# Logits in half steps and q and k for three attention tiles at a time, with an order planned by phase, in a four-layer attention and gMLP kernel

## The chip, the cores and the metric

One core of one Trainium2 chip runs the kernel. The metric is the device time of one execution in microseconds (us). PE is TensorE's matmul row and PEld its weight loads, DVE is VectorE, ACT is ScalarE, POOL is GpSimd, SP is SyncE, which here issues nearly all transfers.

## What is computed

The input x has 2048 rows of 576. Attention A and mixer B alternate, each twice, on the same weights.

```
for two rounds:
    x = x + A(layernorm(x))
    x = x + B(layernorm(x))

A: 32 heads of 18; row s sees keys s, s-2, ..., s-14 (8 keys, 2 apart)
   qkv = x @ wqkv; o = softmax(q . k * 18**-0.5) @ v; return o @ wo
B: z = gelu(x @ w_in)                      # 576 -> 4608
   z1, z2 = halves of z; z2 = layernorm(z2)
   g = w_sp @ z2 + b_sp[:, None]           # over the 2048 rows
   return (z1 * g) @ w_out                 # 2304 -> 576
```

## The kernel before

Five stages follow each other on one core. F0 (`phase_F(0)`) is the first attention and the second half of the first mixer's input product. S1 (`phase_S(1)`) is the mixer's first half and the product over rows with `w_sp`. F2 starts with the mixer's output product (16 row blocks, steps `p3_i`), then does the second attention and again z2. S3 is as S1, and E is the last output product. The change touches F0 and F2 alone.

In an F stage the work is cut into named steps, and class `Flow` puts them in an order. Each step has one or two engines that may take it, a cost, a key (a due time), the steps it comes after, and the buffers that it takes. `Flow.order` keeps a clock for each engine, lets the steps that could start first compete, and takes the one with the least key; a step that stays in the matmul or table mode that the engine is in gets a bonus `STAY`. Then the steps' instructions are issued in that order, so that each engine, and each queue of transfers, works through its list strictly in turn. The costs and keys are numbers in the source: nothing measures them when the kernel is built.

The attention has 18 tiles t of 114 rows (`QT`; 128 with the 14 rows of the window before them). Its steps, with the names that the text uses:

- Layer norm `lnx{i}` (F0), `p3_{i}` (F2), `y{t}` (after the attention): `.s` statistics on DVE, `.p` on POOL, `.n` on ACT, `.t` transpose on PE into `ln_tp`, `.e` copy into the transposed input `xnD`.
- `qk{g}.m0` to `.m4`: q and k of one group of two tiles, 242 columns (`GW`), five blocks of ten matmuls (`mm576`: eight with 128 rows, and two with 64 rows that run side by side). Each block goes to a PSUM tile `qk_ps`, is copied to a staging tile `stg` (`.e0` to `.e4`, six buffers), and written to a bounce tensor in DRAM (`.w0` to `.w4`); step `qk{g}` reads it back in another arrangement into `QK` (three buffers). There are nine groups.
- `v{t}.m`: v of a tile, 20 matmuls on half the array's columns (`v_ps`), and its copy `v{t}`.
- `a{t}.L`: the logits, 64 small matmuls on tiles of 18 rows by 64 columns into two PSUM tiles `L_ps` at once; `.x0` and `.x1` exp on ACT, one for each `L_ps`; `.k` the mask on DVE; `.v` 64 small matmuls into `O_ps`; `.f` divides by the sum (DVE, into `o_t`).
- `w{t}.t` transpose, `.e` copy, `.m0` and `.m1` the product with `wo` (`w_ps`), `.a` the sum with x on DVE, `.w` the store.
- `z{i}.m0` to `.m2`: z2's product for 128 rows, 384 columns each (`z_ps`), `.g0` to `.g2` gelu on ACT, then its layer norm.

All large PSUM tiles come from one ring of three buffers (`H`): `qk_ps`, `v_ps`, `L_ps`, `O_ps`, `w_ps`, `z_ps`, `p3_ps`. The logits of one tile hold two of the three until both exps have read them. Exp and gelu stand in different activation tables; ACT loads a table whenever it goes from one to the other.

The keys before are the same in F0 and F2: a tile's attention has key t (its logits t - 1.2), q and k of group g 2g - 6.5, layer norm ahead of them 2g - 8, v t - 1.5, z2's block i 14.5 + 0.5 i.

Of the kernel before, what the change touches and what calls it, by code (L numbers as in the profile page):

```python
# [11 lines left out]
bf16 = mybir.dt.bfloat16  # L12
# [19 lines left out]
NG = NT // 2  # L32
GW = 2 * QT + HALO
GH = GW // 2
# [6 lines left out]
LX, LW, LR, KQ, KX = 5, 5.0, 6.0, 6.5, 8.0  # L41
# [3 lines left out]
class Flow:  # L45
# [7 lines left out]
    STAY = 0.6  # L53

    def __init__(self, caps):
        self.caps = caps
        self.steps = []
        self.by = {}
        self.users = {}
# [31 lines left out]
    def order(self):  # L91
# [5 lines left out]
        while left:  # L97
# [19 lines left out]
            for e, c in best.items():  # L117
                t0 = max(free.get(e, 0.0), min(t for t, _ in c))
                st = min((st for t, st in c if t <= t0 + 1e-9),
                         key=lambda st: (st["key"] - (self.STAY if self.stays(st, mode.get(e)) else 0), st["n"]))  # L120
                if pick is None or t0 < pick[0]:
                    pick = (t0, e, st)
# [26 lines left out]
class K:  # L149
# [96 lines left out]
    def ln_steps(self, fl, tag, key, row0, n, x, after, uses=(), guard=()):  # L246
# [38 lines left out]
        fl.step(tag + ".s", "DVE", 1.15, key, stats, after, uses, takes=[("ln_st", tag + ".st")])  # L285
        fl.step(tag + ".p", "POOL", 1.2, key, small, [tag + ".s"], [tag + ".st"])
        fl.step(tag + ".n", "ACT", 1.15, key, norm, [tag + ".p"], [tag + ".st", *uses], takes=[("xn", tag + ".xn")])
        fl.step(tag + ".t", "PE", 0.3, key, trans, [tag + ".n"], [tag + ".xn"], takes=[("PT", tag + ".tp")], mode="w")
        fl.step(tag + ".e", ("DVE", "ACT"), 0.72, key, evac, [tag + ".t", *guard], [tag + ".tp"])
# [62 lines left out]
    def phase_F(self, li):  # L352
# [7 lines left out]
        fl = Flow(dict(H=3, PT=2, QK=3, bn=2, stg=6, x=nx, xw=3, xn=3, ln_st=6, o_t=2, oT=2, xb=8))  # L360
# [13 lines left out]
        def QKt():  # L374
            return pool.tile([P, 8, 2, 2, GH], bf16, name="QK", bufs=3)

# [28 lines left out]
        def LNX_steps(i, key):  # L405
            box, tag = {}, f"lnx{i}"

            def load(_):
                box["x"] = pool.tile([P, D], bf16, name="x_in", tag="xb", bufs=8)
                self.dma(box["x"][:], self.A_x[i * P:(i + 1) * P, :])  # L410
            fl.step(tag + ".l", "SP", 0.4, key - 3 if i > 1 else -30, load, takes=[("xb", tag + ".x")], lag=2.2 if i < 2 else LX)
            self.ln_steps(fl, tag, key, i * P, P, lambda: box["x"], [tag + ".l"], [tag + ".x"])
# [8 lines left out]
        def QK_steps(g, key):  # L421
            c0, box, tag = 2 * QT * g, {}, f"qk{g}"

            def opened(_):
                box["bn"] = self.dram.tile([D, 2, 2, GH], bf16, name="qk_bounce", bufs=2)
            fl.step(tag + ".b", "SP", 0.0, key, opened, takes=[("bn", tag + ".bn")])
            for d in range(5):
                M = 126 if d < 4 else 72

                def mm(rest_first, d=d, M=M):  # L430
                    ps = box[d] = self.Ht("qk_ps")
                    cols, at = slice(126 * d, 126 * d + M), slice(c0, c0 + GW)
                    self.mm576(lambda s: ps[:M, s, 0:GW], rest_first,
                               lambda s, c: (wqk[:, c, s, cols], self.xnD[:, c, at]),
                               lambda s, rows: (wqk_r[rows, cols], self.xnD[rows, NM, at]))

                def ev(e, d=d, M=M):
                    stg = box[d, "s"] = pool.tile([P, 2, 2, GH], bf16, name="stg", bufs=6)
                    self.copy(e, stg[:M], box[d][:M, :, 0:GW].rearrange("p q (j r) -> p q r j", r=2))

                def wr(_, d=d, M=M):
                    self.dma(box["bn"][126 * d:126 * d + M], box[d, "s"][:M])
                fl.step(f"{tag}.m{d}", "PE", 1.02, key, mm, feeds(c0, GW) + ["wqk"], takes=[("H", f"{tag}.ps{d}")], mode="wn")
                fl.step(f"{tag}.e{d}", ("DVE", "ACT"), dict(DVE=0.67, ACT=0.58), key, ev, [f"{tag}.m{d}"], [f"{tag}.ps{d}"],
                        takes=[("stg", f"{tag}.s{d}")])
                fl.step(f"{tag}.w{d}", "SP", 0.4, key, wr, [f"{tag}.e{d}", tag + ".b"], [f"{tag}.s{d}", tag + ".bn"],
                        lag=LW)

            def rd(_):
                dst = self.QKs[g] = QKt()  # L450
                heads = box["bn"][:].rearrange("(g r e) q m n -> r e g (q m n)", r=4, e=DH)
                for r in range(4):
                    self.dma(dst[32 * r:32 * r + DH].rearrange("p g q m n -> p g (q m n)"), heads[r])
            fl.step(f"qk{g}", "SP", 1.5, key, rd, [f"{tag}.w{d}" for d in range(5)], [tag + ".bn"],
                    takes=[("QK", f"QK{g}")], lag=LR)
# [3 lines left out]
        def V_steps(t, key):  # L459
# [22 lines left out]
            fl.step(f"v{t}.m", "PE", 1.18, key, mm, feeds(QT * t, P) + ["wv", "fills"] + ([f"a{t - 3}.v"] if t > 2 else []),  # L482
                    takes=[("H", f"v{t}.ps")], mode="ch")
            fl.step(f"v{t}", ("ACT", "DVE"), 0.7, key, ev, [f"v{t}.m"], [f"v{t}.ps"])
# [3 lines left out]
        def ATT_steps(t, key):  # L488
            v, box, Psb = vb[t % 3], {}, Pb[t % 2]
            kb = QH * (t % 2)  # L490
# [3 lines left out]
            def Lm(_):  # L494
                qk = self.QKs[t // 2]
                Ls = box["L"] = [self.Ht("L_ps") for _ in range(2)]
                for g in range(8):
                    for par in range(2):
                        for j in range(4):
                            rows = slice(32 * j, 32 * j + DH)  # L500
                            nc.tensor.matmul(Ls[j // 2][HP * par:HP * par + HP, j % 2, g * QH:(g + 1) * QH],  # L501
                                             lhsT=qk[rows, g, 1, par, kb:kb + HP],
                                             rhs=qk[rows, g, 0, par, kb + HALO // 2:kb + HALO // 2 + QH],
                                             start=True, stop=True, tile_position=(32 * j, HP * par))

            def ex(hh):
                def f(_):
                    nc.scalar.activation(out=Psb[:, 2 * hh:2 * hh + 2, :, 0:QH],  # L508
                                         in_=box["L"][hh][:, :, 0:8 * QH].rearrange("p a (b c) -> p a b c", c=QH),
                                         func=ACT.Exp, scale=SCALE)  # L510
                return f
# [15 lines left out]
            def fin(_):  # L527
# [6 lines left out]
            fl.step(tag + ".L", "PE", 0.55, key - 1.2, Lm, [f"qk{t // 2}"] + ([f"a{t - 1}.L"] if t else []),  # L534
                    [f"QK{t // 2}"], takes=[("H", tag + ".L0"), ("H", tag + ".L1")], mode="q")
            fl.step(tag + ".x0", "ACT", 0.98, key - 1, ex(0), [tag + ".L", "fills"] + ([f"a{t - 2}.v"] if t > 1 else []), [tag + ".L0"],
                    mode="x")
            fl.step(tag + ".x1", "ACT", 0.98, key - 1, ex(1), [tag + ".x0"], [tag + ".L1"], mode="x")
            fl.step(tag + ".k", "DVE", 1.15, key - 0.8, mk, [tag + ".x1", "masks"])
            fl.step(tag + ".v", "PE", 1.05, key - 0.6, pv, [tag + ".k", f"v{t}"] + ([f"a{t - 1}.v"] if t else []),  # L540
                    takes=[("H", tag + ".O")], mode="h")
            fl.step(tag + ".f", "DVE", 1.0, key - 0.4, fin, [tag + ".v"], [tag + ".O"], takes=[("o_t", f"o_t{t}")])
# [36 lines left out]
            def store(_):  # L579
# [4 lines left out]
            fl.step(g + ".e", ("DVE", "ACT"), dict(DVE=0.68, ACT=0.68), key, ev, [g + ".t"], [g + ".tp"], takes=[("oT", g + ".oT")])  # L584
            fl.step(g + ".l", "SP", 0.4, key - 3, load, [] if first else wrote,
                    takes=[("xw", g + ".x")] + ([("xb", g + ".xo")] if first else []), lag=LX if first else 4.0)
            fl.step(g + ".m0", "PE", 0.61, key, wm(0), [g + ".e", "wo"], [g + ".oT"], takes=[("H", g + ".ps")], mode="w")
            fl.step(g + ".m1", "PE", 0.61, key, wm(1), [g + ".m0"], [g + ".oT", g + ".ps"], mode="w")
# [4 lines left out]
            guard += [f"qk{gg}.m{d}" for gg in {t // 2, min(NG - 1, (t + 1) // 2)} for d in range(5)]  # L593
            self.ln_steps(fl, f"y{t}", key + 0.2, QT * t, n, lambda: box["x"], [g + ".a"], [g + ".x"], guard)
# [3 lines left out]
        def Z2_steps(i, key, after):  # L598
# [49 lines left out]
            for u in range(3):  # L648
                fl.step(f"{tag}.m{u}", "PE", 1.54, key, mm(u), need + after, takes=[("H", f"{tag}.ps{u}")], mode="wn")
                fl.step(f"{tag}.g{u}", "ACT", 1.05, key, ge(u), [f"{tag}.m{u}"], [f"{tag}.ps{u}"], mode="g")  # L650
            fl.step(tag + ".q", "DVE", 1.7, key, sqd, [tag + ".g1"])
            fl.step(tag + ".r", "ACT", 0.9, key + 0.5, sqa, [tag + ".g2"])
            fl.step(tag + ".p", "POOL", 2.6, key, small, [tag + ".q", tag + ".r"])
            fl.step(tag + ".n", "DVE", 1.6, key, norm, [tag + ".p"])
# [20 lines left out]
        for i in range(NS):  # L675
            g = next(g for g in range(NG) if 2 * QT * (g + 1) > P * i)
            if first:
                LNX_steps(i, 2 * g - KX)
            else:
                self.p3_steps(fl, i, 2 * g - KX, wout, self.xres[li - 2], li - 1)  # L680
        for g in range(NG):
            QK_steps(g, 2 * g - KQ)
        for t in range(NT):
            V_steps(t, t - 1.5)
# [5 lines left out]
        for i in range(NS):  # L690
            Z2_steps(i, 14.5 + 0.5 * i, [f"win2.{k}" for k in range(len(win2_parts()))] +
# [137 lines left out]
```

## Time and profile before

Three runs took 1280.41, 1284.93 and 1285.19 us; the median is 1284.93. The profiled execution took 1280.8 us, and its span on the core, from the first instruction to the last, is 1278.8 us. The stages below are stretches of that span.

| Stretch | us | PE busy, us | ACT busy, us | DVE busy, us | mean granted clock |
|---|---|---|---|---|---|
| F0, 0 to 257 | 257 | 236.5 | 165.0 | 169.8 | 0.97 |
| S1, 257 to 573 | 316 | 314.2 | 34.7 | 93.7 | 1.00 |
| F2, 573 to 887 | 314 | 304.3 | 169.4 | 184.5 | 0.98 |
| S3, 887 to 1203 | 316 | 314.2 | 34.3 | 93.9 | 1.00 |
| E, 1203 to 1279 | 76 | 70.5 | 10.8 | 14.6 | 1.00 |

The granted clock is TensorE's, as a share of full speed: it is 1 or 0.5, and a mean below 1 says that part of the stretch ran at half. PE counts as busy while any matmul is in flight. Matmuls are pipelined, so the time of a step on PE is read from its first matmul's start to the next step's first start, and not from one matmul's duration.

### The profile page before, as it was taken

Reading aid. Unit: us, or ns where it says so; the run is one execution under the profiler, and the core shown is the slowest. Engines: PE = TensorE matmul, PEld = TensorE weight load, DVE = VectorE, ACT = ScalarE, POOL = GpSimd, SP = SyncE. Lnnn points to the kernel's source line nnn. Section 1 sums busy time; section 2 is a strip of 40 time slices with the busy share of each in tenths; the row PEclk is TensorE's granted clock in tenths of the full one; section 3 lists DMA queues with packets and bytes.
Section 4 is the critical chain, followed back from the end, with each engine's and each line's share of the span. In section 5 each row is a group of like instructions: output and inputs, shape, how many; then the busy total and the mean of one; then the engine's idle time right before and its main releaser. Section 6 shows DMA issues by size and latency. Waiting matters only on the chain.

```text
span 1278.8 us, 27787 instructions
## 1 busy us (share of the span) xinstructions
PE 1239.6 (97%) x12182; PEld 728.2 (57%) x12244; DVE 556.4 (44%) x901; ACT 414.1 (32%) x662; POOL 198.6 (16%) x494
## 2 busy tenths in 40 slices
PE   7999989999999999999999999999999999999998
PEld 6787755444444444448788876554444444444576
DVE  5777666523232323334455675663333232222311
ACT  5744687701111111001435456875100011111011
POOL 5211146700000000001112111575000000000000
PEclk9999899999999999999999998999999999999999
DMA  7655315560000000035545354185300000000232
GB/s 201 165 147 143 87 34 101 122 156 10 10 10 10 10 10 1 1 104 172 148 129 142 110 136 136 34 169 112 99 2 10 10 10 10 10 1 1 79 104 68
DMA packets 142877, 96.31 MB, mean 75 GB/s; under 512 B 92084, under 2 KB 127604, under 8 KB 142756
## 3 DMA queue, kind: packets, MB, share of 16 engines
q1 hardware_dynamic: 142068, 92.17, 28.1%
q0 software_dynamic: 688, 2.38, 0.7%
q8 instruction: 95, 1.56, 0.5%
q14 instruction: 26, 0.21, 0.1%
HBM read 51.19 MB, written 26.55 MB: 61 GB/s over the span
## 4 chain that ended last, share of the span: by engine, by line
PE 89%; DVE 4%; ACT 2%; POOL 2%; issue 1%; DMA 1%; SPq 0%; POOLq 0%; DVEq 0%; ACTq 0%
PE g_ps L746 39%; PE z_ps L241 19%; PE p_ps L316 11%; PE qk_ps L241 6%; PE z_ps L235 3%; PE O_ps L523 3%; PE v_ps L471 3%; PE w_ps L570 2%; PE ln_tp L278 1%; PE qk_ps L235 1%; ACT xn L272 1%; PE o_tp L550 1%; DVE ln_st L256 1%; DVE xw L575 1%; DMA wB<-in_B_w_in_dram 1%
## 5 line engine op out<-in xcount | busy, mean ns | idle before, releaser
L746 PE MATMUL g_ps<-W,zu 128*128 128x512 bf16 x2256 | 497.7, 379 | 2.5
L746 PEld LDWEIGHTS <-zu 128*128 128x128 bf16 x2304 | 225.4, 98 | 271.8
L751 DVE TENSOR_TENSOR g_tmp<-g_ps,bsp 128x512 f32<-128x512 f32 x144 | 99.0, 687 | 437.9 <-PE g_ps L746 437.9
L741 ACT ACTIVATE zu<-z_ps 128x1024 bf16<-128x1024 f32 x72 | 73.7, 1023 | 514.4 <-PE z_ps L235 477.1
L241 PE MATMUL z_ps<-xnD,w 128*128 128x512 bf16 x562 | 132.1, 379 | 1.2 <-issue 0.6
L316 PEld LDWEIGHTS <-zu 128*128 128x128 bf16 x1152 | 111.7, 98 | 31.2 <-DVE zu L752 2.1
L241 PE MATMUL z_ps<-wA,xnD 128*128 128x384 bf16 x576 | 109.9, 327 | 3.9 <-DVE xw L575 3.9
L316 PE MATMUL p_ps<-wA,zu 128*128 128x288 bf16 x768 | 106.0, 286 | 0.5 <-ACT v_ext L296 0.5
L241 PEld LDWEIGHTS <-xnD 128*128 128x128 bf16 x768 | 70.8, 98 | 59.8 <-issue 18.5
L752 DVE TENSOR_TENSOR zu<-g_tmp,zu 128x512 bf16<-128x512 f32 x144 | 99.7, 692 | 9.6
L241 PEld LDWEIGHTS <-w 128*128 128x128 bf16 x576 | 52.7, 97 | 75.2 <-issue 15.7
L241 PE MATMUL qk_ps<-xnD,wqk 128*126 128x242 bf16 (+1 forms) x720 | 91.3, 275 | 2.9 <-DVE o_t L532 1.3
L615 ACT ACTIVATE zu<-z_ps 128x768 bf16<-128x768 f32 x96 | 77.1, 804 | 34.5 <-PE z_ps L235 20.6
L241 PEld LDWEIGHTS <-wqk 128*126 128x126 bf16 (+1 forms) x720 | 76.6, 135 | 10.5 <-issue 7.0
L508 ACT ACTIVATE P<-L_ps 128x912 bf16<-128x912 f32 x72 | 65.0, 943 | 18.1 <-PE L_ps L501 18.0
L625 DVE CUSTOM_DVE_ANT_1 zu<-zu 128x1536 bf16<-128x1536 bf16 x32 | 56.3, 1758 | 29.9 <-ACT zu L615 29.9
L261 POOL TENSOR_SCALAR ln_st<-ln_st 114x1 f32<-114x1 f32 (+1 forms) x68 | 20.1, 296 | 306.7 <-DVE ln_st L257 245.5
L323 DVE TENSOR_TENSOR x<-p_ps,x 128x576 f32<-128x576 f32 x32 | 24.2, 758 | 89.3 <-PE p_ps L316 89.3
L295 DVE CAST stg<-qk_ps 126x484 bf16<-126x484 f32 (+1 forms) x64 | 42.2, 660 | 32.0 <-PE qk_ps L235 20.1
L570 PE MATMUL w_ps<-wo,oT 128*114 128x288 bf16 (+1 forms) x360 | 52.4, 292 | 1.6 <-ACT zu L615 1.4
L471 PE MATMUL v_ps<-wv,xnD 128*64 128x288 bf16 x576 | 46.4, 310 | 1.9 <-DVE o_t L532 1.2
L523 PE MATMUL O_ps<-v_ext,P 64*64 64x19 bf16 x2304 | 43.6, 176 | 4.5 <-issue 1.6
(79 smaller groups left out, 1114.3 us busy)
## 6 DMA issues: line engine op xcount, KB each, us to landing
QK<-qk_bounce SPq DMA_DIRECT2D x72, 136.1 KB
x<-xres SPq DMA_DIRECT2D x32, 288.0 KB
xres<-xw SPq DMA_DIRECT2D x34, 256.5 KB
qk_bounce<-stg SPq DMA_DIRECT2D x72, 119.1 KB
w<-in_B_w_in_dram SPq DMA_DIRECT2D x36, 128.0 KB
xres<-x SPq DMA_DIRECT2D x16, 288.0 KB
xw<-xres SPq DMA_DIRECT2D x17, 256.5 KB
wA<-in_B_w_in_dram SPq DMA_DIRECT2D x12, 288.0 KB
```

The source lines that it names most:

```text
L241: nc.tensor.matmul(ps(s), lhsT=lhsT, rhs=rhs, start=(c == 0 and not rest_first), stop=(c == NM - 1 and rest_first))
L316: nc.tensor.matmul(ps[:, hh, 0:288], lhsT=u[:, s * S + i * P:s * S + (i + 1) * P], rhs=wout(b, s)[:, hh * 288:(hh + 1) * 288], start=(b == ...
L471: self.read_xn_strided(nc.tensor.matmul(ps[HP * par:HP * par + HP, s, 0:288], lhsT=self.xnD[rows, c, c0 + par:c0 + P:2], rhs=wv[:, c, s, : ...
L508: nc.scalar.activation(out=Psb[:, 2 * hh:2 * hh + 2, :, 0:QH], in_=box["L"][hh][:, :, 0:8 * QH].rearrange("p a (b c) -> p a b c", c=QH), f ...
L523: nc.tensor.matmul(O[rows, h // 16, (h % 16) * (DH + 1):(h % 16 + 1) * (DH + 1)], lhsT=Psb[rows, h % 4, h // 4, :], rhs=v[rows, h, :], sta ...
L570: nc.tensor.matmul(box["ps"][:n, hh, 0:288], lhsT=box["oT"][:, c, :n], rhs=wo[:, c, hh * 288:(hh + 1) * 288], start=(c == 0), stop=(c == 4))
L615: nc.scalar.activation(out=self.zu[:, 3 * u:3 * u + 3, 256 * i:256 * (i + 1)].rearrange("p j (s r) -> p s j r", s=2), in_=box[u][:, :, 0:3 ...
L625: nc.vector.tensor_tensor_reduce(out=junk(0, 6), in0=z[:, 0:6, :], in1=z[:, 0:6, :], scale=1.0 / FH, scalar=0.0, op0=ALU.mult, op1=ALU.add ...
L741: nc.scalar.activation(out=u[:, :, 512 * q:512 * (q + 1)], in_=ps[:], func=ACT.Gelu_apprx_tanh)
L746: nc.tensor.matmul(ps[:, s, :], lhsT=z2[:, i, s, :], rhs=W[q][:, i, :], start=(i == 0), stop=(i == NS - 1))
L751: nc.vector.tensor_tensor(out=tmp[:], in0=ps[:, s, :], in1=bsp[:, 512 * q:512 * (q + 1)], op=ALU.add)
L752: nc.vector.tensor_tensor(out=uv, in0=tmp[:], in1=uv, op=ALU.mult)
```

## The change

1. **Groups.** q and k are made for three tiles at a time (356 columns) in most groups: F0 has groups of 2, 2, 2, 3, 3, 3, 3 tiles, F2 six groups of 3. `QK` has two buffers instead of three, each 1.47 times as wide; `stg` has four buffers instead of six, each wide enough for 356 columns.
2. **Logits.** `a{t}.L` becomes `a{t}.La` (heads of row tiles 0 and 1) and `a{t}.L` (row tiles 2 and 3), 32 matmuls each, each with one `L_ps` buffer. `.x0` needs `La` alone.
3. **Keys and costs.** The keys' offsets, `STAY` and the assumed landing times come from a table with one row for F0 and one for F2. Most costs are new numbers too. z2 is due two units later (16.5 instead of 14.5), the layer norm ahead of q and k in F2 3.6 units earlier.

No arithmetic changes. As built, the order on the engines moves with it: on PE 24,490 rows become 23,990, on SP 320 become 296.

```diff
+GROUPS = ((2, 2, 2, 3, 3, 3, 3), (3, 3, 3, 3, 3, 3))
+GH = (max(max(g) for g in GROUPS) * QT + HALO) // 2
-LX, LW, LR, KQ, KX = 5, 5.0, 6.0, 6.5, 8.0
+Plan = namedtuple("Plan", "LX LW LR KQ KX KV KL KE KM KP KF KY KZ STAY")
+PLANS = (Plan(LX=4.32, LW=3.65, LR=6.57, KQ=5.69, KX=7.91, KV=1.19, KL=1.2, KE=1.43, KM=1.14, KP=1, KF=0, KY=1.02,
+              KZ=16.53, STAY=0.39),
+         Plan(LX=3.66, LW=4.24, LR=8.75, KQ=5.56, KX=11.63, KV=1.48, KL=1.95, KE=0.47, KM=0.75, KP=0.6, KF=1.6, KY=1.28,
+              KZ=16.55, STAY=0.48))
...
-        fl = Flow(dict(H=3, PT=2, QK=3, bn=2, stg=6, x=nx, xw=3, xn=3, ln_st=6, o_t=2, oT=2, xb=8))
+        sizes = GROUPS[0 if first else 1]
+        t0s = [sum(sizes[:g]) for g in range(len(sizes))]
+        group = [g for g, n in enumerate(sizes) for _ in range(n)]
+        pl = PLANS[0 if first else 1]
+        fl = Flow(dict(H=3, PT=2, QK=2, bn=2, stg=4, x=nx, xw=3, xn=3, ln_st=6, o_t=2, oT=2, xb=8), pl.STAY)
...
-            return pool.tile([P, 8, 2, 2, GH], bf16, name="QK", bufs=3)
+            return pool.tile([P, 32 * GH], bf16, name="QK", bufs=2)
...
-            c0, box, tag = 2 * QT * g, {}, f"qk{g}"
+            c0, gw, box, tag = QT * t0s[g], QT * sizes[g] + HALO, {}, f"qk{g}"
...
-                    stg = box[d, "s"] = pool.tile([P, 2, 2, GH], bf16, name="stg", bufs=6)
+                    t = pool.tile([P, 4 * GH], bf16, name="stg", bufs=4)
+                    stg = box[d, "s"] = t[:, 0:2 * gw].rearrange("p (q r j) -> p q r j", q=2, r=2)
...
-                fl.step(f"{tag}.m{d}", "PE", 1.02, key, mm, feeds(c0, GW) + ["wqk"], takes=[("H", f"{tag}.ps{d}")], mode="wn")
+                fl.step(f"{tag}.m{d}", "PE", 0.2 + 0.0039 * gw, key, mm, feeds(c0, gw) + ["wqk"],
+                        takes=[("H", f"{tag}.ps{d}")], mode="wn")
...
-            def Lm(_):
-                qk = self.QKs[t // 2]
-                Ls = box["L"] = [self.Ht("L_ps") for _ in range(2)]
-                for g in range(8):
-                    for par in range(2):
-                        for j in range(4):
+            def Lm(a):
+                def f(_):
+                    qk = self.QKs[group[t]]
+                    ps = box["L", a] = self.Ht("L_ps")
+                    for g in range(8):
+                        for par in range(2):
+                            for j in (2 * a, 2 * a + 1):
...
-            fl.step(tag + ".L", "PE", 0.55, key - 1.2, Lm, [f"qk{t // 2}"] + ([f"a{t - 1}.L"] if t else []),
-                    [f"QK{t // 2}"], takes=[("H", tag + ".L0"), ("H", tag + ".L1")], mode="q")
+            fl.step(tag + ".La", "PE", 0.34, key - pl.KL, Lm(0), [f"qk{group[t]}"] + ([f"a{t - 1}.L"] if t else []),
+                    [f"QK{group[t]}"], takes=[("H", tag + ".L0")], mode="q")
+            fl.step(tag + ".L", "PE", 0.34, key - pl.KL, Lm(1), [tag + ".La"], [f"QK{group[t]}"], takes=[("H", tag + ".L1")],
+                    mode="q")
...
-            fl.step(tag + ".v", "PE", 1.05, key - 0.6, pv, [tag + ".k", f"v{t}"] + ([f"a{t - 1}.v"] if t else []),
+            fl.step(tag + ".v", "PE", 1.1, key - pl.KP, pv, [tag + ".k", f"v{t}"] + ([f"a{t - 1}.v"] if t else []),
...
-            QK_steps(g, 2 * g - KQ)
+            QK_steps(g, t0s[g] - pl.KQ)
...
-            Z2_steps(i, 14.5 + 0.5 * i, [f"win2.{k}" for k in range(len(win2_parts()))] +
+            Z2_steps(i, pl.KZ + 0.5 * i, [f"win2.{k}" for k in range(len(win2_parts()))] +
```

## The prediction

> **What bounds the kernel now.** I read the page first: the busy shares, the clock row and the chain that ended last.
>
> ```profile
> span 1278.8 us, 27787 instructions
> ...
> PEclk9999899999999999999999998999999999999999
> ...
> PE 89%; DVE 4%; ACT 2%; POOL 2%; issue 1%; DMA 1%; SPq 0%; POOLq 0%; DVEq 0%; ACTq 0%
> ```
>
> 89% of the chain is PE's own work. So a change can win in three ways only: less work on PE, less waiting of PE, or fewer stretches in which TensorE is granted half its clock. The next view sums PE over stretches of F0 and F2 that I cut where the order changes character (columns: stretch, length, PE busy with its matmuls, granted clock, DMA share, GB/s).
>
> ```profile
> 35.00:127.00 92.00, 87.22 (x2018) 0.96 0.59 153
> 127.00:152.00 25.00, 22.22 (x664) 0.88 0.42 107
> 152.00:200.00 48.00, 43.61 (x727) 0.99 0.11 31
> 630.00:740.00 110.00, 109.19 (x2122) 1.00 0.46 126
> 740.00:757.00 17.00, 16.12 (x329) 0.90 0.44 123
> 757.00:790.00 33.00, 29.66 (x814) 0.84 0.58 152
> 790.00:825.00 35.00, 31.72 (x452) 1.00 0.20 60
> ```
>
> By the step order these are: attention with q and k matmuls between (35 to 127, 740 to 757), attention alone, "bare" (127 to 152, 757 to 790), attention mixed with z2 (152 to 200, 790 to 825), and attention filled with the output product (630 to 740). PE idles 4.8 + 2.8 + 4.4 + 0.8 + 0.9 + 3.3 + 3.3 = 20.3 us in them. At half clock they lose at most 92 x 0.04 + 25 x 0.12 + 48 x 0.01 + 17 x 0.10 + 33 x 0.16 = 14.2 us. Next, who is waited for in F0 (35 to 200):
>
> ```profile
> PE z_ps L241 <- DVE xw L575: 1.9, 2, 1.0
> PE qk_ps L241 <- DVE o_t L532: 1.3, 1, 1.3
> PE v_ps L471 <- DVE o_t L532: 1.2, 1, 1.2
> PE O_ps L523 <- ACT P L508: 1.1, 1, 1.1
> ```
>
> None of these waits is for data (the products of q, k, v and z2 read neither `o_t` nor `xw`, and the `O_ps` held at 133.3 belongs to an earlier tile's exps): it is the ring of three PSUM buffers. In the timeline the last three and a wait of 0.6 at 99.9 stand right behind a tile's logits, which hold two buffers, while the third waits to be emptied.
>
> **The clock.** Two of the six drops, each with the stretch before it:
>
> ```profile
> 81.00:84.40 3.40, 2.12 (x112) 1.00 0.67 145
> 84.40:87.80 3.40, 3.40 (x24) 0.50 0.71 156
> 132.20:135.60 3.40, 2.13 (x133) 1.00 0.67 140
> 135.60:139.00 3.40, 3.40 (x43) 0.50 0.55 122
> ```
>
> Ahead of each PE idled 1.3 us and did the small matmuls of `L_ps` and `O_ps`. A drop lasts 3.4 us and costs at most 1.7. Three of the six follow one of the waits behind logits (84.4, 111.7, 135.6).
>
> **Part 1, wider groups.** Two pairs of steps in the chain in order of time:
>
> ```profile
> 593.42 1.80 PE qk_ps L241 x16
> 595.22 0.35 PE qk_ps L235 x4
> 595.56 1.80 PE qk_ps L241 x16
> ```
>
> Two blocks of 242 columns take 2.14, so 1.07 each; z2's blocks of 384 columns come at 216.21 and 219.35, 1.57 each. 356 columns by the line between: 1.07 + 114/142 x 0.50 = 1.47. Before, 90 x 1.07 = 96.3; after, 15 x 1.07 + 50 x 1.47 = 89.6: **-6.7**. Ends: -1.5 if a block grows with its columns (1.07 x 356/242 = 1.57), -9 if it stays 0.05 under the line. SP issues 25 writes and 20 reads fewer at some 0.33 us each; its queue lies beside PE, no credit.
>
> Four staging buffers instead of six: `.e4` of a group waits until `.w0` has landed. The chain has such a landing at 7.39 ("DMA qk_bounce<-stg", at 23.64) and ACT's timeline shows a copy held 4.26 us by it, in spite of six buffers. Elsewhere the read-back issues 4.5 us after the last write (91.1 to 95.7). A buffer's turn is copy 0.92 (0.66 grown by 228 of 484 elements, most of it), issue 0.31, landing, 0.1. At 4.5 it is 5.8; from m0's end to m4's in the new order I count 6.2 to 7.7 us of PE steps, so the ten wide groups hide it. At F0's start, where 15 blocks of 1.07 follow each other almost unbroken, four buffers turn in 5.6 to 8.5 us against 4.8 of PE steps. Both ends: 0 to +10 there. I take **+1.5**, since six buffers cost PE only 2.6 idle us in 10 to 80.
>
> `QK` with two buffers holds six tiles as before. In the new order at least 18 us of PE steps lie between the logits that free a buffer and those that need its next content, and 13.6 (F0) and 16.8 (F2) between the first group's last block and its logits, against some 12 for a landing, four issues and a read: 0. With that cover gone, each us of delay on SP's queue, where later writes and x loads stand behind the read, would be a us of PE.
>
> **Part 2, half logits.** The page gives 64 logits matmuls 25.8/36 = 0.72 busy, and 64 of `O_ps` 43.6/36 = 1.21; start to next start 0.64 and 1.11. Logits run on eight tiles side by side, `O_ps` on two, a half step on four. So a pair of halves lies between 16 rounds at `O_ps`'s 35 ns, 0.56, and 1.11: -2.9 to +16.9 us for 36 tiles. A quarter of the tiles costs `O_ps` only 1.7 times the time, so the pace comes mostly from issue; I take 0.68, **+1.4**. The Trainium skill (TensorE: Matmul & The Clock Gate, Part 3: Packing small matmuls) puts the gain of small matmuls in how many tiles run side by side; by that, half as many tiles would double the time, +23 us. The `O_ps` row disagrees, but no run shows four.
>
> Entering small matmuls costs: ten of `w_ps` take 1.36 to the next start ahead of `v_ps` (669.25 to 670.61) and 1.22 ahead of `qk_ps` (680.56 to 681.78). The step orders have 64 entries before and 53 after: 11 x 0.13 = **-1.4**.
>
> What the halves free: the first exp may start 0.3 us sooner and `La` may start with one buffer free. The waits behind logits are 1.3 + 1.2 + 1.1 + 0.6 + 0.3 (762) = 4.5, and the three drops behind them at 1.4 another 4.2. If two thirds go: **-6**. Ends 0 and -9.
>
> **Part 3, the order.** z2 moves behind the last tiles: 30 z2 steps lie ahead of the last `O_ps` before, 4 after. So the mixed stretches shrink, ACT changes tables once a phase (14 loads of 1.28 us before), and the bare stretches grow. In PE work by the rows above (F0 / F2, us): with q and k 73.8 / 14.8 before, 72.4 / 54.1 after; bare 22.1 / 28.9, then 35.4 / 36.8; mixed 38.1 / 31.3, then 4.0 / 5.9; filled 109 in F2, then 52, as F2 does nine blocks of output product ahead of everything. At each stretch's own idle rate (6.5%, 12.6%, 11.5% in F0; 6%, 11.6%, 10.5%, 0.7% in F2) PE would idle 9.7 + 8.5 = 18.2 against 20.3: -2.1. At each one's own clock loss it loses 3.6 + 4.8 in F0 and 3.3 + 6.7 in F2, 18.4 against 14.2: +4. Together **+1.9**: by itself the reordering only moves the waits. The new costs are nearer the rows (v 1.36 against 1.35 measured, `.f` 1.14 against 1.11, `oT` 0.83 against 0.82; before 1.18, 1.0, 0.68), so steps should be placed less early: of some 4 us in waits under 0.7 I credit half, **-2** (ends 0 and -8).
>
> **Sum:** -6.7 + 1.5 + 1.4 - 1.4 - 6 + 1.9 - 2 = -11.3. The span and the 2.0 us around it make 1280.8; 1280.8 - 11.3 = 1269.5, **1269**. The median of the three runs lies 4.1 above the profiled one; the range carries that.
>
> **Rivals.**
> - *Waits mostly go.* Three quarters of 20.3 + 0.8 x 14.2 = 31.7 go, 24, with -6.7 of work: 1250. For it: the ring is named in the largest waits. Against it: bare attention grows. 0.16.
> - *The ring stays the bound*, the halves being issued back to back in 33 of 36 tiles: -6 and -2 fall away, 1277.5. 0.12.
> - *Staging stalls, slower.* If landings are 7.4 everywhere, a turn is 8.7, and `.e4` is late by 1.0 to 2.5 us, mean 1.9, in ten groups, 19, and the start by 11 x (8.5/4 - 1.2) = 10. ACT and DVE are in order: behind the held copy wait masks, `o_t` and exps, so PE pays it. 1269 + 27.5 = 1296. It decides from landings of some 6 us on. For it: the 4.26 us wait; against: 4.5 in mid-phase. 0.09.
> - *Drops vanish.* The six drops come after 0.6 to 1.3 idle us with small matmuls around. [...] If the new order had none, some 11 us go: 1258. 0.02.
> - *Tiles set the pace of logits*: each half takes 0.64, +23 - 1.4: 1291. For it: nothing but that four tiles were never run. 0.03.
>
> **Chances.** Forecast 0.58. Half a percent, 6.4 us, is about what a measurement here can tell from no change, so faster means under 1278.5. Of the forecast's share 0.54 is faster, 0.04 same; the ring rival splits 0.04 and 0.08, the tile rival 0.01 same and 0.02 slower. Faster 0.54 + 0.16 + 0.02 + 0.04 = 0.76; same 0.13; slower 0.11. The range 1249 to 1286 holds the forecast with its unknown ends (-8 to +10, and 4 for the median) and the ring rival; half of the first rival, the slow ones and tails make the 0.2 outside.
>
> **What would show it.** Right: `qk_ps` blocks of 356 columns at 1.47; pairs of halves at 0.68; no exp beside gelu, and two table loads a phase; PE's waits behind `L_ps` for `o_t` gone; PE idle in F0 and F2 down by some 5 us; four to six half-clock windows. Wrong: `stg` copies waiting for "DMA qk_bounce<-stg" by more than 3 us in all on the chain; logits at 1 us; bare stretches with over 12% idle or a drop every ten us.

## The result, and the profile after

Six runs of the changed kernel took 1291.30 to 1299.08 us, median 1295.53; six of the kernel before, beside them, 1279.22 to 1285.19, median 1281.28. The ratio is 1.0117, with a 95% interval of 1.0098 to 1.0136: the change costs about 15 us, and the prediction of 1269 us, range 1249 to 1286, was wrong in sign. One run of e7 and one of e14, each over 1.5% above the fastest of its kernel, are left out of all numbers below.

The page of the profiled execution (1295.94 us): its span, the row of granted clocks, the chain that ended last.

```profile
span 1294.2 us, 27174 instructions
...
PEclk9699999999999999999999798999999999999999
...
PE 92%; issue 2%; DMA 2%; DVE 2%; ACT 1%; POOL 0%; SPq 0%; DVEq 0%; ACTq 0%; POOLq 0%
```

Two things are new. The clock row has a 6 in the second slice and a 7 in the 23rd (704 to 740 lies there), and in the chain DMA and "issue" (time in which PE waited for nothing that the profile shows) have each gone from 1% to 2%. The stretches say where (columns: stretch, length, PE, PEld, DVE, ACT and POOL busy, granted clock, DMA share, GB/s):

```profile
14.00:34.00 20.00, 14.88 (x151) 12.30 (x150) 11.02 (x30) 9.99 (x18) 14.04 (x42) 0.99 0.69 169
34.00:54.00 20.00, 17.97 (x276) 12.83 (x276) 11.34 (x23) 13.05 (x21) 5.25 (x12) 0.50 0.57 139
54.00:127.00 73.00, 65.80 (x1574) 53.80 (x1573) 46.98 (x80) 35.32 (x50) 10.59 (x27) 0.97 0.53 139
127.00:152.00 25.00, 24.55 (x525) 20.02 (x523) 17.31 (x29) 12.03 (x18) 2.67 (x6) 0.89 0.44 119
704.00:740.00 36.00, 29.09 (x581) 23.28 (x578) 17.23 (x29) 13.47 (x19) 3.67 (x9) 0.81 0.38 100
740.00:790.00 50.00, 41.97 (x1024) 33.90 (x1025) 30.39 (x49) 25.10 (x36) 6.54 (x17) 0.95 0.57 146
```

Twenty us at the start of F0 run wholly at half clock; from 704 to 790 PE idles 6.9 + 8.0 = 14.9 us, and the clock drops there as well. Next, what PE waited for, largest sums first, and the two rows of the copies that were themselves held (total us, times, longest):

```profile
PE L_ps L516 <- issue: 10.9, 7, 4.3
PE ln_tp L283 <- ACT xn L277: 7.9, 4, 6.2
PE O_ps L539 <- issue: 5.5, 5, 2.5
PE qk_ps L246 <- ACT stg L301: 5.0, 1, 5.0
PE O_ps L539 <- DVE stg L300: 3.8, 2, 3.3
```

```profile
DVE stg L300 <- DMA qk_bounce<-stg: 14.0, 4, 5.0
...
ACT stg L301 <- DMA qk_bounce<-stg: 8.5, 1, 8.5
```

The waits named in the prediction (`z_ps` and `v_ps` for a DVE that held a ring buffer) are gone from the top. In their place stand 5.0 + 3.8 = 8.8 us behind `stg` and 10.9 + 5.5 = 16.4 us of "issue", of which the profile before has 1.6 us, at one place.

**The copy that is held.** The chain in order of time at the start of F0, and the clock there:

```profile
25.39 0.43 DVE stg L300
25.82 8.49 DMA qk_bounce<-stg
...
34.41 0.57 ACT stg L301
...
35.02 1.77 PE qk_ps L246 x8
```

```profile
30.30:33.70 3.40, 0.00 (x0) 0.00 (x0) 0.00 (x0) 0.00 (x0) 1.05 (x3) 1.00 0.78 185
33.70:54.20 20.50, 18.17 (x276) 12.97 (x276) 11.34 (x23) 13.05 (x21) 5.39 (x12) 0.50 0.57 139
...
781.20:784.65 3.45, 1.35 (x67) 1.11 (x64) 2.73 (x5) 2.40 (x3) 0.00 (x0) 1.00 0.84 183
784.65:794.90 10.25, 8.06 (x168) 6.47 (x169) 3.15 (x5) 3.11 (x5) 1.05 (x3) 0.50 0.68 146
```

This place lies in F0's groups of two (copies of 126 x 484). A write of q and k issued at 25.82 takes 8.49 us to land; the copy that needs its tile waits till 34.4, and PE, whose ring is full of uncopied products, does nothing from 30.3 to 33.7. Half clock for 20.5 us follows. The Trainium skill (TensorE: Matmul & The Clock Gate, Part 1) has the clock fall after an idle window of about 3.4 us; this drop agrees. Others do not need one: from 781.2 to 784.65 PE was busy for 1.35 us, mostly with small matmuls, and 10.2 us at half clock followed.

In F2 it is the queue. The timeline around 710 (start, us, what):

```profile
707.83 0.90 DVE L300 CAST stg<-qk_ps 126x712 bf16<-126x712 f32 x1 [1.08 <-PE qk_ps L246]
...
709.99 0.26 SPq L169 DMA_DIRECT2D xw<-xres  x1
710.34 0.34 SPq L169 DMA_DIRECT2D xres<-x  x1
710.73 2.58 SPq L169 DMA_DIRECT2D qk_bounce<-stg  x4
...
716.22 0.90 DVE L300 CAST stg<-qk_ps 72x712 bf16<-72x712 f32 x1 [4.21 <-DMA qk_bounce<-stg]
```

The first copy of this group ended at 707.08 (ACT), but SP, working in order, issued its write only at 710.73, behind an `xw` load and an `xres` store. So the fifth copy waits 4.2 us for its tile, and the weighted values, which need the ring buffer that it would empty, wait 3.3. Half clock follows here too, from 716.4 to 723.2.

**The stalls called "issue".** One of them, in the middle of a tile's logits:

```profile
725.79 0.44 PE L516 MATMUL L_ps<-QK 18*64 18x57 bf16 x29 [0.22 <-DVE o_t L548]
729.58 0.26 PE L516 MATMUL L_ps<-QK 18*64 18x57 bf16 x3 [3.35 <-issue]
```

Counted in PE's program (matmuls, loads and a few semaphore instructions), 13 of the 17 gaps of over 0.3 us inside a tile's logits or weighted values, 18.7 us from start to next start beyond the usual pace, come at instructions whose number leaves 194 or 195 divided by 256; the other four are of 0.4 to 0.56 us, with a releaser. The page's row "q8 instruction: 93, 1.52, 0.5%" has 93 packets of 16 kB; 23,990 PE rows in 93 packets are 258 each. So PE stops at the border of a block of its own program until the next has come; e3 below tests that.

### The profile page after: what moved, and what is told of

Read it like the earlier page. It is cut to its first block, busy times and chain, and to the rows that moved or that the text cites. A ratio compares the mean times of both kernels' runs of the same rounds, so it can differ in the third digit from the quotient of the medians.

```text
span 1294.2 us, 27174 instructions
## 1 busy us (share of the span) xinstructions
PE 1243.0 (96%) x11932; PEld 723.7 (56%) x11994; DVE 546.8 (42%) x876; ACT 405.9 (31%) x652; POOL 197.1 (15%) x494
## 3 DMA queue, kind: packets, MB, share of 16 engines
q1 hardware_dynamic: 135788, 91.84, 27.6%
q8 instruction: 93, 1.52, 0.5%
## 4 chain that ended last, share of the span: by engine, by line
PE 92%; issue 2%; DMA 2%; DVE 2%; ACT 1%; POOL 0%; SPq 0%; DVEq 0%; ACTq 0%; POOLq 0%
PE g_ps L764 38%; PE z_ps L246 20%; PE p_ps L321 11%; PE qk_ps L246 5%; PE v_ps L485 4%; PE w_ps L588 4%; PE z_ps L240 3%; PE O_ps L539 3%; DMA qk_bounce<-stg 2%; PE L_ps L516 2%; PE ln_tp L283 1%; PE o_tp L568 1%; PE qk_ps L240 1%; ACT xn L277 1%; DMA x_in<-in_A_x_dram 0%
## 5 line engine op out<-in xcount | busy, mean ns | idle before, releaser
L246 PEld LDWEIGHTS <-w 128*128 128x128 bf16 x576 | 52.9, 97 | 75.1 <-issue 15.3
L246 PE MATMUL qk_ps<-xnD,wqk 128*126 128x356 bf16 (+3 forms) x520 | 89.0, 317 | 6.1 <-ACT stg L301 5.0
L246 PEld LDWEIGHTS <-wqk 128*126 128x126 bf16 (+1 forms) x520 | 64.6, 137 | 20.7 <-issue 11.9
L266 POOL TENSOR_SCALAR ln_st<-ln_st 128x1 f32<-128x1 f32 (+1 forms) x68 | 19.5, 287 | 345.2 <-DVE ln_st L262 311.5
L300 DVE CAST stg<-qk_ps 126x712 bf16<-126x712 f32 (+3 forms) x48 | 40.5, 850 | 40.7 <-DMA qk_bounce<-stg 14.0
L588 PE MATMUL w_ps<-wo,oT 128*114 128x288 bf16 (+1 forms) x360 | 56.0, 308 | 1.8 <-ACT xn L277 1.1
L539 PE MATMUL O_ps<-v_ext,P 64*64 64x19 bf16 x2304 | 46.2, 178 | 9.6 <-issue 5.5
L277 ACT ACTIVATE xn<-xw,ln_st 114x512 bf16<-114x512 f32 (+1 forms) x72 | 43.0, 646 | 30.5 <-POOL ln_st L268 28.7
```

The lines of the kernel that those rows point to most:

```text
L246: nc.tensor.matmul(ps(s), lhsT=lhsT, rhs=rhs, start=(c == 0 and not rest_first), stop=(c == NM - 1 and rest_first))
L277: nc.scalar.activation(out=out, in_=in_, func=ACT.Identity, scale=rstd[:n], bias=nmr[:n])
L539: nc.tensor.matmul(O[rows, h // 16, (h % 16) * (DH + 1):(h % 16 + 1) * (DH + 1)], lhsT=Psb[rows, h % 4, h // 4, :], rhs=v[rows, h, :], sta ...
L588: nc.tensor.matmul(box["ps"][:n, hh, 0:288], lhsT=box["oT"][:, c, :n], rhs=wo[:, c, hh * 288:(hh + 1) * 288], start=(c == 0), stop=(c == 4))
```

## The experiments

All sixteen, in the order run. "Clock loss" is the mean over the runs of span x (1 - mean granted clock), "rest" the mean of span x clock. Clock loss is the most that the half clock can have cost: at half clock PE also waits for other engines and for transfers, and such a wait need not be longer for it.

| Kernel | median us | ratio to before, 95% | rest, us | clock loss, us |
|---|---|---|---|---|
| before (122 runs beside the others) | 1279.4 to 1281.5 | 1 | 1268.3 | 10.2 |
| changed | 1295.53 | 1.0098 to 1.0136 | 1266.3 | 27.6 |
| e1 more staging | 1283.16 | 0.9992 to 1.0053 | 1260.2 | 21.6 |
| e2 before, shifted | 1279.66 | 0.9984 to 1.0020 | 1267.3 | 11.0 |
| e4 halves alone | 1297.49 | 1.0092 to 1.0167 | 1272.7 | 23.0 |
| e5 wide alone | 1288.46 | 1.0036 to 1.0089 | 1271.1 | 16.4 |
| e6 wide + keys | 1287.86 | 1.0032 to 1.0085 | 1262.9 | 22.8 |
| e7 keys alone | 1276.83 | 0.9948 to 0.9996 | 1259.7 | 14.9 |
| e8 halves + wide | 1311.25 | 1.0180 to 1.0260 | 1271.4 | 37.3 |
| e9 before, four staging | 1285.75 | 1.0012 to 1.0047 | 1270.8 | 12.4 |
| e10 halves + keys | 1279.73 | 0.9965 to 1.0020 | 1261.7 | 16.1 |
| e11 e1, spread | 1278.03 | 0.9951 to 1.0018 | 1261.3 | 16.9 |
| e12 e10, spread | 1276.18 | 0.9937 to 0.9998 | 1260.8 | 14.0 |
| e13 e7, spread | 1279.26 | 0.9969 to 1.0014 | 1263.1 | 15.0 |
| e14 more staging in F0 | 1287.14 | 1.0020 to 1.0074 | 1262.0 | 22.6 |
| e15 F0 of e1, F2 of e7 | 1282.99 | 0.9991 to 1.0046 | 1261.3 | 19.4 |
| e16 e15, F0 spread | 1289.76 | 1.0045 to 1.0098 | 1268.4 | 19.0 |

e3, a tail behind the kernel before, stands below.

**Staging (e1, e9, e14).**

```diff
-                    t = pool.tile([P, 4 * GH], bf16, name="stg", bufs=4)
+                    t = pool.tile([P, 4 * GH], bf16, name="stg", bufs=5 if first else 6)
...
-                rec = pool.tile([P, 2, 16], f32, name="rec", bufs=2)
+                rec = pool.tile([P, 2, 16], f32, name="rec", bufs=1)
```

e14 has 5 and 4; e9 is the kernel before with 4 for 6.

> The changed kernel, its order untouched, with more staging tiles behind the copies: five in the first attention phase (one `rec` tile given up for the room) and six in the second, in place of four; the planner is still told four. Theory 'staging': the copies no longer wait for the write four copies earlier, so PE's waits for `stg` (5.0 us at 30 us, 3.3 us at 714 us) go, with the 20.5 us at half clock behind the first: 1295.5 - 5.0 - 10 - 3.3 - 2 = about 1275, at most 1283. Theory 'instruction fetch': only that part goes, and PE's stalls with 'issue' in the middle of the small matmuls keep their sum of about 18 us and their places. Rival 'it is the order': the gaps reappear elsewhere, at the clock or at the QK read, and the time stays above 1290.

> The kernel before with four staging tiles behind the copies instead of six, its order and all else untouched: the cost of the staging by itself, under groups of two. The prediction gave +1.5 us (0 to +10). Theory 'staging': at the start of the first attention phase a copy waits for the write four copies earlier, PE stalls for a few us and the clock falls behind it: 1284-1290. Rival 'four are enough for groups of two (968 bytes a partition each, short writes)': 1280 +- 2.

> The changed kernel with five staging tiles in the first attention phase and the four of the change in the second; six there gave 1283, four in both 1295.5. Theory 'staging': the wait at 30 us and the half clock behind it are gone (about -15 at most in a single profile, of them 10 clock), and the wait of 3.3 us at 714 us with its drops of 13.6 us stays (+3 to +8 against 1283): 1285-1291. Rival 'the first phase is all': 1283 +- 2. Rival 'the second phase is most': 1291 or more.

With more tiles the change takes 1283.16: 12.4 us come back, half of them as rest (6.1), half as clock (6.0). The stretches of e1's profile that answer to those above:

```profile
14.00:34.00 20.00, 16.05 (x165) 13.75 (x165) 11.71 (x31) 13.76 (x25) 13.85 (x42) 1.00 0.71 177
34.00:54.00 20.00, 19.60 (x388) 15.48 (x389) 14.89 (x31) 10.61 (x16) 7.08 (x17) 0.83 0.69 171
```

They are of e1's second fastest run (1274.52). In F2 the wait is gone ("PE O_ps L539 <- DVE stg L300: 0.4, 1, 0.4" is what is left behind `stg`), though SP issues the first write of the same group as late as before (693.23, its copy ended at 690.42): with six tiles the fifth copy need not wait for it. In F0 a wait stays: "PE v_ps L485 <- DVE stg L300: 4.0, 1, 4.0" ends at 33.9, behind a copy that waited 4.06 us for a landing. So the fifth tile took 1 us from PE's wait of 5.0, and the 20.5 us at half clock behind it became 6.8. The forecast that this wait would go was wrong, and that F0's gain comes from the wait is not shown; the medians show only that the tile wins it. e14 lies between e1 and the changed kernel, so F0's tile wins some 8 us and F2's two some 4; the intervals of e14 and e1 overlap, and the split is no better than that. e9 puts four tiles at +4.7 us under groups of two and the old keys; the other 7.7 need the wide groups or the new order, and which of them is not shown.

e1 and e14 run the same PE program as the changed kernel, yet the stalls at block borders sum to 10.7 and 13.5 us in their profiles, not 18.7. Theory 'instruction fetch' had their sum stay; only the places in the blocks did.

**Instruction blocks (e2, e3).**

```diff
+        hd = self.Ht("head_ps")
+        for k in range(64):
+            nc.tensor.matmul(hd[0:HP, 0, 0:QH], lhsT=self.ident[0:DH, 0:HP], rhs=self.ident[0:DH, 0:QH], start=True, stop=True)
```

> The kernel before with 64 more small matmuls (128 instructions with their loads) on PE right after `ident` is made, when PE has nothing to do yet; nothing else changes, and every later PE instruction moves half a block of 256 instructions. Theory 'instruction fetch' (PE stalls at the border of a block of 256 where the block held less than about 4 us of work): summed over its blocks, the kernel before lacks 6.8 us against 4 us a block, the shifted one 15.5 us, with nine blocks under 3 us instead of three. So 'issue' stalls rise from 1.8 us to between 5 and 10 us, at other instructions than now, all at the same remainder of 256, and the time to 1284-1292. Rival 'a stall belongs to its step' (a semaphore, a tile position, a bank): the one stall of 1.8 us at 780 us stays where it is and the time stays at 1281 +- 2.

> The kernel before with 1024 matmuls of the logits' shape (18 x 64 by 57) behind the last matmul of the last phase, on tiles that nobody reads: 2048 PE instructions, eight blocks of 256. Theory 'instruction fetch': each block runs its 128 matmuls in 1.3 us and then stands still until the next is fetched, so a block takes 3 to 4 us and the lot 24-32 us, with a gap at every 128th matmul. Rival: the stalls have another cause, and the lot runs at the logits' 10 ns a matmul, 10 us without gaps.

The one run takes 1302.49 us, 22.7 more than the kernel before, where work without stops would add 10. Its timeline (start, us, what; idle before it):

```profile
1281.04 1.33 PE L775 MATMUL tail_ps<-ident 18*64 18x57 bf16 x128 [2.79 <-issue]
1284.51 1.33 PE L775 MATMUL tail_ps<-ident 18*64 18x57 bf16 x128 [2.14 <-issue]
```

128 matmuls with their loads are 256 instructions; they run 1.33 us and stand still for 2.14, and so on to the end. The page of this run has 103 packets of queue q8 against 95 before: eight more for eight blocks. Here a block takes 3.47 us, at half clock (granted 0.50 from 1281 to 1300) and with a DMA share of 0.02. That is no fixed floor: in the changed kernel a block that ended in such a stall took 2.9 us (to 74.92), another 7.1 (779.70 to 786.84). The shift shows the same from the other side: the stall of 1.6 us at 780 (1.80 from start to start) is gone, others of 1.46, 0.76 and 0.42 us came at other steps, again at 194 or 195 of 256. But their sum did not rise to 5 us, nor the time (1279.66): counting how much each block lacks against 4 us foretells neither. The Trainium skill (Runtime: NRT & Kernel Launch, Instruction fetch mechanics) has the next 256 instructions fetched while the current ones execute, mostly hidden. That holds in S1 of the kernel before, where PE is busy 314.2 of 316 us; these rows contradict it for runs of logits and weighted values.

**The three parts, apart and together (e4 to e8, e10).** Each is the kernel before or after with the named part put in or out. Wide groups come with two `QK` buffers instead of three, five staging tiles in F0 and six in F2 (six in both with groups of two), one `rec` tile, and an order planned for four staging tiles; no run parts them.

> The kernel before with the logits in two half steps and nothing else of the change: groups of two, three wide buffers, six staging tiles and the old keys. The prediction gave the halves -6 us from the waits for the ring and +1.4 us of PE time: 1277. Theory 'instruction fetch': the blocks lack 10.9 us against 4 us instead of 6.8, so one or two more 'issue' stalls, +1 to +3: 1275-1282. Theory 'the halves do the harm': above 1288, with most of the 18 us of 'issue' stalls of the changed kernel here.

> The wide groups alone: groups of two and three, two wide buffers, the logits in one step of 64, the keys and costs of before; five and six staging tiles so that the staging is out of the comparison. The prediction gave the groups -6.7 us of PE time and -1.4 for fewer entries: 1272 if nothing else moves. Theory 'instruction fetch': its blocks lack 15.8 us against 4 us instead of 6.8, worth about +3: 1275. Theory 'the groups starve the logits' (a group of three must land whole before its first tile, with two buffers instead of three): PE waits for QK in both attention phases, 1285 or more.

> Everything of the change but the halves: wide groups, new keys and costs, the logits in one step; five and six staging tiles. Theory 'the halves do harm under any keys' (they cost +17 us alone): 1283 - 17 = 1266. Theory 'the halves and the new keys need each other' (the halves cost under the old keys, where the planner keeps a ring tile for a logits half whose exponential comes late; the new keys were laid out for them): without the halves the new keys lose, 1285 or more. Theory 'instruction fetch' alone: the blocks lack 24.7 us against 29.2 with the halves, so 1-2 us less than the changed kernel with more staging: 1281.

> The new keys and costs alone: groups of two, three buffers, six staging tiles, the logits in one step. The prediction gave the reordering +1.9 and the costs -2: 1281. Theory 'instruction fetch': the blocks lack 19.6 us instead of 6.8, so some 4 to 8 us of 'issue' stalls and the clock behind them: 1284-1292. Theory 'the new keys are what wins back': below 1277.

> Halves and wide groups under the old keys and costs, five and six staging tiles; against the changed kernel with more staging (1283) only the keys and costs are put back. Theory 'the halves do harm under the old keys': the halves' +17 and the groups' -8 make 1289-1290. Theory 'the order by the new keys does the harm' (its blocks lack 29.2 us, here 19.4): 1276 or less.

> The change without the wide groups: halves, new keys and costs, groups of two, three buffers, six staging tiles. The halves cost +17 alone, +23 on the wide groups with the old keys, and won 5 on the wide groups with the new keys (1288 to 1283). Theory 'halves and new keys need each other': the same gain on the new keys alone, 1277 - 5 = 1272. Theory 'what the halves win under the new keys is only the room they give the wide groups': no gain here, 1277 or more.

The parts do not add. Under the old keys the halves cost 17.7 us alone and 22.8 on top of wide groups (e5 to e8); under the new keys they cost 2.9 (e7 to e10) or win 4.7 (e6 to e1). Of e4's 17.7 at most 12.8 are clock; e4's profile has 3.9 us of stalls at borders, not the 18 that its theory had. That halves and new keys need each other came out with wide groups (e6) and not with groups of two (e10); why the halves do so much harm under the old keys is not shown. The new keys win 3.4 alone. Wide groups cost in all four pairs: 8 (before to e5), 14 (e4 to e8), 11 (e7 to e6) and 3.4 (e10 to e1, where the intervals overlap). That they starve the logits is not the reason: no wait of PE for `QK` stands in e5's list. One way from before to the change is then keys -3.4 (by e7's ratio -3.6), halves +2.9, wide groups +3.4, and four staging tiles +12.4: 15.3 in all. Another way gives other shares.

**Spreading the small matmuls (e11, e12, e13, e15, e16).** The planner got one term more in its choice:

```diff
+    def thin(self, st, e):
+        if e != "PE" or st["mode"] not in ("q", "h"):
+            return 0
+        n, us = self.COUNT[st["mode"]], st["cost"]
+        for m, c in reversed(self.past):
+            if n >= self.BLOCK:
+                break
+            n, us = n + m, us + c
+        return self.THIN if us < self.ENOUGH else 0
```

> The changed kernel with more staging, and one rule more in the planner: a step of logits or of weighted values that would leave the last 256 PE instructions with less than 4.4 us of work steps back by 2 in its key, so that other ready work goes between. Blocks under 3 us fall from 13 to 3, the lack against 4 us from 29.2 to 11.2; the planner's own span grows by 4.9 and 3.3 us. Theory 'clusters of small matmuls cost, through the fetch and through the clock': 'issue' stalls at block borders from 10.6 us to 3 or less, the mean clock from 0.983 up to 0.988 or more: 1283 - 7 - 6 + up to 8 = 1270-1278. Rival 'the clock falls for PE's waits, not for clusters': stalls fewer, clock as it was, time 1283 or more.

> The change without the wide groups, with the same rule (3.6 us instead of 4.4): the lack against 4 us goes from 21.1 to 11.7 us, the planner's span by -0.8 and +3.3 us. Theory 'clusters cost': 4 to 8 us faster than the run without the rule, below 1270. Rival 'the order by keys matters more than the clusters': no faster than the run without the rule.

> The new keys and costs on the old tiles (groups of two, logits in one step, six staging tiles), with the rule that keeps steps of logits and weighted values apart (3.4 us, 1.5 in the key): against 3.5 us a block the lack falls from 11.6 to 1.0 us, one block under 3 us instead of ten; the planner's span grows by 1.5 and 0.9 us. Theory 'clusters cost, through fetch and clock': 'issue' stalls at borders from 7 us to about 1, the clock's loss from 15.7 us (over the runs without the rule) to about 11: 1277 - 5 - 4 + 2 = about 1270, ratio under 0.994. Rival 'the spread gives back in waits what it saves': 1277 or more.

> Each attention phase with what served it best in the profiles so far: the first with halves, wide groups, new keys and five staging tiles (240 to 244 us in three profiles, before 250.5), the second with the new keys alone, groups of two, one logits step and six staging tiles (302.5 us, before 307.0). Theory 'the phases add': 1280.8 - 7 - 4.5 = 1269. Rival 'the short first phases were lucky profiles' (the medians of those kernels lie 9 to 12 us above their profiled runs, and the lower clock decides it): no gain from the first phase, 1276-1278, as with the new keys alone.

> As the one with each phase its own, and in the first phase the rule that keeps small matmuls apart (4.4 us, 2.0 in the key): there the blocks lack 9 us against 4 us instead of 16. Theory 'clusters cost through the clock': the first phase's loss of clock falls from some 12 to some 6 us: 3 to 6 us faster than without the rule. Rival 'the rule changes nothing at the median': within 2 us of it.

These settle little in favour of the theory. e11 and e12 lie 5.1 and 3.6 us under their twins without the rule, within what such medians scatter; e11's stalls fell from 10.7 to 6.5 us where 3 or less was expected, and e12 missed its 1270. e13 lies 2 above its twin, with 5.7 us of stalls at borders in its profile where 1 was expected; e16 lies 7 above e15, all of it rest. So the stalls are real, but what of the 18.7 us reached the end is not shown: keeping small matmuls apart may put other waits in their place. e15's miss (1282.99 for 1269) shows how little one profile tells: the F0 (up to S1's first matmul) that e1 and e14 ran in 243.5 and 240.3 us took 262.7 in e15's profile, in the same order with the same buffers, 37.5 us of it at half clock; the wait behind `stg` at its start was 3.3 us there. e7 and e12 are the best of all (1276.83 and 1276.18, some 0.3% under before, interval just clear of 1); nothing with wide groups got clear of it.

## Why the prediction was wrong

- **Wider groups, -6.7.** The work was right. Two blocks at full clock in the chain of the changed kernel:

```profile
54.80 1.21 PE qk_ps L246 x8
56.01 0.45 PE qk_ps L240 x4
56.45 1.35 PE qk_ps L246 x8
57.80 1.23 PE w_ps L588 x10
```

  3.00 for two, 1.50 each against 1.47; summed from start to next start, with half clock taken out, q and k fell from 100.4 to 94.4 us. What failed is that the sum took work saved as time saved. In all four pairs wide groups, with what comes with them, made the kernel slower or left it the same: rest moved by +2.8 (e5), -1.3 (e8), +3.2 (e6) and -1.5 (e1), and clock loss rose by 5.5 to 14.
- **Staging, +1.5: the step of the sum that failed most.** It measured +12.4: some 8 at F0's start, priced at 1.5 out of 0 to 10, and some 4 in F2, where the ten wide groups were to hide it at no cost. I took a landing of 4.5 us and let the steps from m0 to m4 hide a turn of 5.8. The landing that mattered in F0 took 8.49; in F2 the write left 3.65 us late from SP's queue, which I had as "beside PE, no credit", and landed 5.37 later; and up to half of the price was clock, which the term lacked. These two landings, 13.9 us on the chain, are the sign of being wrong that the prediction named. The rival *Staging stalls, slower* gave 1296 and has the right cause, but by another sum: two places with PE waits of 5.0 and 3.3 us and the half clock behind them, not ten groups late by 1.9. That its number came so near is luck.
- **Halves, +1.4 and -6.** The work was right (logits from 23.7 to 25.3 us, +1.6; a pair shows as 0.70 for its 64), so the rival *Tiles set the pace* is out. The waits behind logits went. But nothing was won: e10 against e7 is +2.9, rest +2.0 and clock loss +1.2. I had taken it that waits which go leave time behind; what took it up is not shown.
- **Order, +1.9, and costs, -2.** Together 0 in the sum, -3.6 by e7's ratio: rest -8.6, clock loss +4.7. The idle fell by twice the 4 us that the two had for it, and the clock came near the +4. That is in part luck: e7 has groups of two, and so not the order that was priced. And the +4 holds a slip: at the rate of its own stretch the first of F2's clock terms is 1.7 x 54.1/14.8 = 6.2 and not 3.3, which makes it +7.
- **The clock: +4 in the order, -4.2 in the halves, about 0.** It measured 27.6 against 10.2 us, +17.4, more than the whole loss, since rest fell by 2.0. Of it 6.0 go with the staging, 5.5 with the wide groups, 1.2 with the halves and 4.7 with the keys (e1, e10, e7 in turn). So the sum lacked the clock that staging and wide groups bring, and the halves gave none back. It also took a drop to last 3.4 us; one of the six before lasts 10.2 (from 777.3), and the one at F0's start after the change 20.5.
- **"Issue", not in the sum.** I passed over 1.6 us in the list of before. The stalls went to 18.7 in one profile; their share of the 15 us is open.

## What to carry to other kernels

Where a buffer is made wider and fewer, trace the whole turn of one buffer, from the copy through the queue ahead of its write to the landing at its worst place, and put the clock behind a stall into its price. Saved work on the busiest engine counts only in stretches where that engine has no waits; here 6 us less work never came out as time. A program of hundreds of small matmuls in a row can also stand still until its own instructions arrive, and here its clock fell after a stretch in which PE was busy for only 1.35 of 3.45 us: look for both before making large matmuls fewer.

## What the runs showed of the hardware

- One program's time follows the clock that it happens to get. e15's twelve runs go from 1272.25 (mean clock 0.989) to 1289.47 (0.980), while span x clock has a standard deviation of 2.5 us. A single profile of such a kernel says little about its median: e14's was its fastest run, 11.6 us below.
- PE can wait for its own instructions. In a tail of 18 x 64 by 57 matmuls each 256 instructions, 128 pairs of load and matmul, took 3.47 us at granted clock 0.50, 1.33 of them work. The same PE program had 18.7, 13.5 and 10.7 us of such stalls in three profiles.
- Logits on four tiles of the array run nearly as fast as on eight (25.3 us for 2304 matmuls against 23.7).
